# Regrouping the attention cycles of a fused transformer block: five cycles of six or seven exponentials per group in place of six of five or six

## The chip, the cores and the metric

The kernel runs on one core of one Trainium2 chip. The metric is the time of one execution on the device, in microseconds (us). Three runs of the kernel before took 1409.46, 1410.82 and 1412.63 us, so the median is 1410.82 us.

The engines are named as the profile names them: PE is TensorE's matmul, PEld its weight load, ACT is ScalarE, DVE is VectorE, POOL is GpSimd and SP is SyncE, which here only issues DMAs.

## The reference

The reference is one pre-norm transformer block on 2048 rows of width 512: attention with 32 query heads of width 16 that share a single key head and a single value head, then a gated feed-forward part with 1792 hidden columns.

```python
h  = x + A(layernorm(x), wq, wk, wv, wo)
h2 = h + B(layernorm(h), w_gate, w_up, w_down)

def A(x, wq, wk, wv, wo):            # q: 32 heads of 16; one k, one v of width 16
    scores = einsum("bhqd,bkd->bhqk", q, k) * 16 ** -0.5
    p = softmax(scores)
    return merge_heads(einsum("bhqk,bkd->bhqd", p, v)) @ wo

def B(x, w_gate, w_up, w_down):
    return (gelu(x @ w_gate) * (x @ w_up)) @ w_down     # tanh form of gelu
```

## The kernel before, in words

The 2048 query rows are cut into four blocks of 512 (`NB`, `T`), the 32 heads into eight groups of four (`NG`), the 2048 keys into sixteen chunks of 128 (`KC`). For one block, one group and one key chunk, the kernel makes the 128 x 512 scores of four heads, takes their exponential into a tile `p` (128 x 4 x 512), and adds `v` times `p` into an accumulator `acc` that holds the four heads of the group.

PE work of the attention comes in two kinds. A **score** (`scores`, line 431) is a pair of matmuls for two heads: the two run at once on the two halves of PE's rows, and one ACT instruction (line 435) turns the 128 x 1024 result into half of a `p` tile. So a chunk needs two scores and two exponentials, and a group needs 32 of each. A **weighing** (`weigh`, line 439) takes one whole `p` tile and adds it into `acc`: four products on four column strips of PE, 32 columns wide. In PSUM there are two score tiles (tag `s`, two banks each), one bank for `acc`, and three banks for other products. Score number n therefore can't begin until exponential n - 2 has left the score tile that it reuses. There are five `p` tiles (`PB = 5`).

While the scores of block b + 1 are made, the same loop also makes the **dense products** of block b: the output projection, the layer norm's transposes, the gate, up and down products. A generator (`dense`) yields after every dense step, and the loop asks for steps. In the main part of it (`weave`, line 949) a step is again a pair of matmuls, one on each half of PE's rows.

The order on PE, ACT, DVE and SP is the order in which the program is written. It is made by the loop at line 1165, which goes through **cycles**. A cycle emits a few scores, with a written number of dense steps behind each (`shares`), and ends with the weighings of all `p` tiles that are complete (`finish`, line 1021): those whose last exponential isn't the one just issued, and at a group's end all that are left. `SIZES` holds the number of scores of the six cycles of a group, 6, 5, 5, 6, 5 and 5. In the long middle stretch of a block (kind `"woven"`) the shares are these; the last row is that of a group's last cycle:

```python
WOVEN = {6: (0, 6, 3, 3, 2, 0), 5: (0, 6, 3, 2, 0)}
LAST = (0, 6, 4, 2, 0)
```

`(0, 6, 3, 3, 2, 0)` reads: two scores, six dense steps, a score, three steps, a score, three steps, a score, two steps, a score, then the weighings. A block has 36 woven cycles; ahead of them stand four `"long"` ones and a `"gap"`, behind them four `"long"` and two `"short"` ones.

At a cycle's end `open_gates` puts the tanh of a finished gate product (line 826) into ACT's order, and one entry of `outs` (the division of a finished group) goes to `lazy`. `soon` and `lazy` hold DVE instructions; one of them is emitted behind each score (line 1192).

Of the kernel before, what the change touches and what calls it, by code (L numbers as in the profile page):

```python
# [54 lines left out]
RUNS = ((0, 1, 2, 3), (4, 5, 6, 7), (8, 9, 10, 11), (12, 13))  # L55

BOUND_STEPS = ((0, 10), (0, 14))

CUT, EDGE, GAP, HOLD, REST = -1, -2, -3, -4, -5

# [2 lines left out]
def kernel(  # L63
# [21 lines left out]
    NB = S // T  # L85
# [3 lines left out]
    NG = H // 4  # L89
    KC = S // P  # L90
# [69 lines left out]
    def attend(first):  # L160
        with ExitStack() as outer:
            with tc.manual_schedule(
                engines={mybir.EngineType.PE, mybir.EngineType.Pool, mybir.EngineType.Activation}
            ):
                run(outer, first)


    def run(outer, first):
# [268 lines left out]
        def weigh(acc, p, kc):  # L437
            for j in range(4):
                nc.tensor.matmul(  # L439
                    acc[32 * j : 32 * j + 32, :], v_sb[:, kc, :], p[:, j, :],  # L440
                    start=(kc == 0), stop=(kc == KC - 1), skip_group_check=True,
                )
# [3 lines left out]
        def take_out():  # L446
            for step in outs.pop(0):
                step()
# [570 lines left out]
        pend = []  # L1019

        def finish(n):
            for _ in range(min(n, len(pend))):
                pb, pg, pkc, pp, pacc, _ = pend.pop(0)
                weigh(pacc, pp, pkc)
                if pkc == KC - 1:
                    evacuate(pb, pg, pacc)
# [5 lines left out]
        def open_gates():  # L1032
            while gates:
                gates.pop(0)()
# [9 lines left out]
        def score(n, beside=()):  # L1044

            nonlocal acc
            i, u = divmod(n, 2)
            b, r = divmod(i, PER)
            g, kc = divmod(r, KC)
            if u == 0:  # L1050
                if kc == 0:
                    cur["qg"] = qgs.pop((b, g))
                    acc = pss.tile([P, T], F32, tag="acc", bufs=1, name=f"acc_{b}_{g}")
                if kc == 2 and b * NG + g + 1 < NB * NG:
                    key = divmod(b * NG + g + 1, NG)
                    qgs[key] = load_q(*key)
                cur["p"] = sb.tile([P, 4, T], F32, tag="p", bufs=PB, name=f"p_{i}")
            scores(i, cur["p"], cur["qg"], kc, u, beside)
            if u == 1:
                pend.append((b, g, kc, cur["p"], acc, n))  # L1060
# [9 lines left out]
        SIZES = (6, 5, 5, 6, 5, 5)  # L1070

        LEAD = (3, 2, 2)
        n, lead = 0, 2 * PER + sum(SIZES[: LEAD[0]])
        with tc.manual_schedule(engines={mybir.EngineType.SP, mybir.EngineType.DVE}):
# [79 lines left out]

        WOVEN = {6: (0, 6, 3, 3, 2, 0), 5: (0, 6, 3, 2, 0)}
        LAST = (0, 6, 4, 2, 0)
        kinds = (
            ["long"] * 4 + ["gap"] + ["woven"] * 6 * len(SIZES) + ["long"] * 4 + ["short"] * 2
        )
        todo = list(kinds)  # L1160
        fixed = ExitStack()
        fixed.enter_context(
            tc.manual_schedule(engines={mybir.EngineType.SP, mybir.EngineType.DVE})
        )
        for c in range(LEAD[0], (NB - 1) * NG * len(SIZES)):
            b, cb = divmod(c, NG * len(SIZES))
            if first and (b, cb) in BOUND_STEPS:
                bound_flag(BOUND_STEPS.index((b, cb)))
            cg = cb % len(SIZES)
            size, kind = SIZES[cg], None  # L1170
            if b > 0 and cb == LEAD[b]:
                assert work is None
                work, todo = dense(b), list(kinds)
            if work is not None:
                kind = todo.pop(0)
            if kind == "long":
                shares = LONG[size]
            elif kind == "woven":
                shares = LAST if cg == len(SIZES) - 1 else WOVEN[size]
            elif kind == "short":  # L1180
                shares = SHORT[size]
            else:
                shares = PLAIN[size]
            due, said = 0, None
            if kind != "woven":
                while lazy:
                    lazy.pop(0)()
            for j, share in enumerate(shares):
                score(n)
                n += 1  # L1190
                if soon or lazy:
                    (soon or lazy).pop(0)()  # L1192

                if b > 0 and cb == 1 and j == 3 and outs:
                    take_out()

                if kind in (None, "gap") and n % 2 == 0:
                    finish(sum(e[5] < n - 1 for e in pend))
                if kind == "gap" and j == 1:

                    said = next(work)
                due += share
                while due > 0:
                    said = next(work)
                    if said > 0:
                        due -= 1
                    elif said == CUT and kind != "short":
                        break

            ends = kind not in (None, "woven") or kind == "woven" and todo[0] != "woven"  # L1210
            while ends and said not in (CUT, GAP):
                said = next(work)
                assert said < 0, said
            open_gates()
            if work is not None and not todo:
                assert next(work, None) is None
                work = None
            finish(sum(e[5] < n - 1 for e in pend) if cg < len(SIZES) - 1 else len(pend))
            while behind:
                behind.pop(0)()  # L1220
            if outs and kind == "woven":
                lazy.extend(outs.pop(0))
            elif outs:
                take_out()
# [266 lines left out]
    def bound_flag(step):  # L1491
        if step == 0:
            nc.gpsimd.dma_start(b2, b_d)
            return
        nc.vector.tensor_reduce(b1, b2, axis=AX.X, op=ALU.max)

        nc.vector.tensor_scalar(flag, b1, (BOUND_MAX / SCALE) ** 2, None, op0=ALU.is_le)
# [69 lines left out]
```

## Time and profile before

| what | value |
|---|---|
| median of three runs | 1410.82 us (1409.46 to 1412.63) |
| span of the profiled execution, first to last instruction | 1408.1 us |
| PE busy, share of the span | 1391.7 us, 99% |
| ACT busy | 1041.2 us, 74% |
| DVE busy | 552.7 us, 39% |
| score pairs, exponentials | 1024 of each |
| groups 2 to 6 of block 2 (from 700.05 to 901.98 us) | 201.93 us for five groups |

The profile is that of one execution; its own time is known as its span, 1408.1 us, which leaves out what lies ahead of the first instruction and behind the last. The span is 1.4 us under the fastest of the three runs and 2.7 us under their median. PE's matmuls are pipelined and the profile models their ends, so "busy" on PE doesn't mean that PE works at its peak: the starts of successive matmuls say how long a step took. A line such as `s<-qg,kaug` names the tile written and the tiles read; `50*128` behind it are the rows and columns of PE that the matmul holds.

### The profile page before, as it was taken

The page shows a single profiled execution, that of the slowest core. Times are in us where ns is not written, and L with a number is a line of the kernel's source. Part 1 is how long each engine was busy: PE and PEld are TensorE (multiplying, and loading weights), DVE is VectorE, ACT ScalarE, POOL GpSimd, SP SyncE. Part 2 cuts the span into 40 slices and gives each one's busy share as a digit, 9 for nine tenths or more (in the row PEclk, how much of TensorE's full clock was granted, in tenths as well). Part 3 has the DMA queues.
Part 4 walks back from the last instruction along what each step waited for, and adds up shares of the span by engine and source line. Part 5 has one row for each costly group of instructions (what it writes and reads, how often), then busy time and mean ns, then how long its engine had stood idle before and what let it go on. Part 6 is the DMA issues. An engine that isn't in the chain of part 4 may idle for free.

```text
span 1408.1 us, 25648 instructions
## 1 busy us (share of the span) xinstructions
PE 1391.7 (99%) x10646; PEld 782.7 (56%) x10646; DVE 552.7 (39%) x982; ACT 1041.2 (74%) x1149; POOL 189.4 (13%) x288
## 2 busy tenths in 40 slices
PE   8999999999999999999999999999999999999998
PEld 7433333335555555555555655555555555557886
DVE  7322323333342434333252433424352342427665
ACT  7699999996777787777787777777787777772000
POOL 6655565501000000000000000001000000002000
PEclk9999999999999999999999999999999999999999
DMA  4578777842341322233252332223242241335551
GB/s 160 162 238 273 236 243 243 298 134 91 126 150 53 124 106 102 73 112 122 84 169 72 117 118 87 87 100 111 99 151 97 88 147 56 134 124 198 181 199 59
DMA packets 85041, 194.52 MB, mean 138 GB/s; under 512 B 9904, under 2 KB 24240, under 8 KB 84884
## 3 DMA queue, kind: packets, MB, share of 16 engines
q1 hardware_dynamic: 77484, 167.39, 35.3%
q0 software_dynamic: 7264, 25.30, 5.0%
q8 instruction: 86, 1.41, 0.4%
q14 instruction: 39, 0.32, 0.1%
q10 hardware_dynamic: 168, 0.10, 0.0%
HBM read 142.93 MB, written 49.55 MB: 137 GB/s over the span
## 4 chain that ended last, share of the span: by engine, by line
PE 93%; ACT 3%; DMA 1%; issue 1%; DVE 1%; POOL 0%; SPq 0%; ACTq 0%; DVEq 0%; POOLq 0%
PE acc L439 33%; PE s L431 19%; PE pu L949 9%; PE pg L949 8%; PE pd L949 4%; PE pq L429 4%; PE pd L626 3%; ACT p L435 3%; PE pd L648 3%; PE pg L648 3%; PE pu L648 3%; PE pp L626 2%; PE pp L757 1%; DMA x<-in_A_x_dram 1%; PE pxt L693 1%
## 5 line engine op out<-in xcount | busy, mean ns | idle before, releaser
L435 ACT ACTIVATE p<-s 128x1024 f32<-128x1024 f32 x1024 | 969.7, 1030 | 224.6 <-PE s L431 220.1
L439 PE MATMUL acc<-p,v_sb 128*32 128x512 f32 x4096 | 496.4, 600 | 0.0
L431 PE MATMUL s<-qg,kaug 50*128 50x512 f32 x1984 | 416.3, 423 | 3.7 <-ACT p L435 3.6
L431 PEld LDWEIGHTS s<-qg,kaug 50*128 50x128 f32 x1984 | 194.6, 184 | 217.8 <-ACT p L435 120.6
L439 PEld LDWEIGHTS acc<-p,v_sb 128*32 128x32 f32 x4096 | 109.8, 109 | 229.2 <-issue 226.0
L949 PE MATMUL pu<-x2h,w 64*128 64x512 f32 x672 | 211.8, 391 | 0.0
L949 PE MATMUL pg<-x2h,w 64*128 64x512 f32 x672 | 211.5, 391 | 0.1
L949 PEld LDWEIGHTS pu<-x2h,w 64*128 64x128 f32 x672 | 115.8, 185 | 15.1
L949 PEld LDWEIGHTS pg<-x2h,w 64*128 64x128 f32 x672 | 116.2, 185 | 12.6 <-DVE g L823 0.5
L949 PE MATMUL pg<-x2l,w 64*128 64x512 f32 x336 | 122.2, 391 | 0.0
L949 PE MATMUL pu<-x2l,w 64*128 64x512 f32 x336 | 121.8, 390 | 0.0
L826 ACT ACTIVATE ga<-ga 128x512 f32<-128x512 f32 x56 | 35.3, 634 | 89.2 <-DVE ga L821 89.2
L139 POOL TENSOR_SCALAR rstd<-mv 128x1 f32<-128x1 f32 x16 | 3.5, 221 | 666.4 <-DVE mv L137 666.4
L949 PE MATMUL pd<-w,gh 64*128 64x512 f32 x384 | 81.3, 392 | 0.0
L891 DVE TENSOR_TENSOR h<-h,pd 128x512 f32<-128x512 f32 x48 | 31.9, 685 | 115.4 <-PE pd L949 66.4
L1192 DVE SCALAR_TENSOR_TENSOR ga<-ga,g 128x512 f32<-128x512 f32 x70 | 48.3, 691 | 52.3 <-ACT ga L826 51.2
L452 DVE COPY oT<-acc 128x512 f32<-128x512 f32 x32 | 22.1, 692 | 112.1 <-PE acc L439 111.9
L479 DVE RECIPROCAL oc<-oc 128x128 f32<-128x128 f32 x64 | 56.3, 921 | 24.3 <-DMA oc<-acc_d 19.5
L810 DVE COPY g<-pg 128x512 f32<-128x512 f32 x56 | 38.8, 692 | 62.8 <-PE pg L949 57.0
L949 PEld LDWEIGHTS pu<-x2l,w 64*128 64x128 f32 x336 | 57.9, 185 | 7.6
L949 PEld LDWEIGHTS pg<-x2l,w 64*128 64x128 f32 x336 | 58.1, 185 | 6.1
L823 DVE SCALAR_TENSOR_TENSOR g<-g,pu 128x512 f32<-128x512 f32 x56 | 38.2, 683 | 40.4 <-PE pu L949 30.4
(248 smaller groups left out, 1462.4 us busy)
## 6 DMA issues: line engine op xcount, KB each, us to landing
w<-w_d SPq DMA_DIRECT2D x112, 512.0 KB
w<-w_d SPq DMA_DIRECT2D x28, 1024.0 KB
qg<-q_d SPq DMA_DIRECT2D x46, 200.0 KB
q_d<-qh SPq DMA_DIRECT2D x32, 256.0 KB
wo<-wo_d SPq DMA_DIRECT2D x8, 1024.0 KB
acc_d<-oT SPq DMA_DIRECT2D x31, 256.0 KB
oc<-acc_d SPq DMA_DIRECT2D x124, 64.0 KB
w_d<-w_0b POOLq DMA_DIRECT2D x14, 512.0 KB, 7.6
```

Of the source, the lines that this page charges most:

```text
L429: step()
L431: nc.tensor.matmul(s[:, a, :], kaug[rows, kc * P : (kc + 1) * P], qg[rows, 2 * u + a, :], start=True, stop=True,)
L435: nc.scalar.activation(p[:, 2 * u : 2 * u + 2, :], s, AF.Exp, scale=SCALE)
L439: nc.tensor.matmul(acc[32 * j : 32 * j + 32, :], v_sb[:, kc, :], p[:, j, :], start=(kc == 0), stop=(kc == KC - 1), skip_group_check=True,)
L479: nc.vector.reciprocal(oc[:, 1, sl], oc[:, 1, sl])
L626: nc.tensor.matmul(banks[k], lhsT[rows], rhs[rows], start=(turn == 0 and i == 0), stop=(turn == 1 and i == n - 1), skip_group_check=True,)
L648: nc.tensor.matmul(bank, lhsT, rhs, start=(i == 0), stop=(i == len(ts) - 1))
L810: nc.vector.tensor_copy(g, pg)
L823: nc.vector.scalar_tensor_tensor(g, g, 0.5, pu, op0=ALU.mult, op1=ALU.mult)
L826: nc.scalar.activation(a, a, AF.Tanh, scale=GELU_A * GELU_C)
L949: nc.tensor.matmul(e["bank"], lhsT[rows], rhs[rows], start=i == 0 and not e["both"], stop=last and e["both"], skip_group_check=True,)
L1192: (soon or lazy).pop(0)()
```

## The change

The change touches five of the eight groups in each of blocks 1 to 3, numbered from 0: groups 2 to 6 (`FULL`). For those, a group is cut into five cycles of 7, 6, 7, 6 and 6 scores, with the dense steps given by the new table `WIDE`. Their number per group stays: 73 before (14 + 11 + 11 + 14 + 11 + 12) and 73 now (16 + 13 + 16 + 14 + 14). Groups 0, 1 and 7 keep their six cycles. The number of woven cycles of a block falls from 36 to 31, and a cycle's place in its group comes from a list (`rows`) in place of a division.

```diff
+FULL = range(2, 7)
...
         WOVEN = {6: (0, 6, 3, 3, 2, 0), 5: (0, 6, 3, 2, 0)}
         LAST = (0, 6, 4, 2, 0)
+        WIDE = (
+            (0, 4, 3, 3, 3, 3, 0), (0, 4, 3, 3, 3, 0), (0, 4, 3, 3, 3, 3, 0),
+            (0, 5, 3, 3, 3, 0), (0, 5, 3, 3, 3, 0),
+        )
+        assert sum(map(len, WIDE)) == 2 * KC
+        rows = []
+        for g in range(NG):
+            sizes = [len(w) for w in WIDE] if g in FULL else SIZES
+            rows.extend(
+                (g, cg, size, cg == len(sizes) - 1) for cg, size in enumerate(sizes)
+            )
+        spare = len(SIZES) - len(WIDE)
         kinds = (
-            ["long"] * 4 + ["gap"] + ["woven"] * 6 * len(SIZES) + ["long"] * 4 + ["short"] * 2
+            ["long"] * 4 + ["gap"] + ["woven"] * (6 * len(SIZES) - spare * len(FULL))
+            + ["long"] * 4 + ["short"] * 2
         )
...
-        for c in range(LEAD[0], (NB - 1) * NG * len(SIZES)):
-            b, cb = divmod(c, NG * len(SIZES))
+        for c in range(LEAD[0], (NB - 1) * len(rows)):
+            b, cb = divmod(c, len(rows))
...
-            cg = cb % len(SIZES)
-            size, kind = SIZES[cg], None
+            g, cg, size, final = rows[cb]
+            kind = None
...
-                shares = LAST if cg == len(SIZES) - 1 else WOVEN[size]
+                shares = WIDE[cg] if g in FULL else LAST if final else WOVEN[size]
...
-            finish(sum(e[5] < n - 1 for e in pend) if cg < len(SIZES) - 1 else len(pend))
+            finish(len(pend) if final else sum(e[5] < n - 1 for e in pend))
```

Two places show what this does to PE's order, both in the first cycle of group 2 of block 2 (the one that begins at 700.05 us in the profile before). `s_` are score matmuls (x2 is one score), `pg_` and `pu_` are gate and up products (two rows are one dense step), `acc_` are weighings (x4 is one `p` tile).

The first place is the stretch between the second and the third score of the cycle. Before, its last five dense steps and the third score:

```order
L949 MATMUL pg_2_7461<-x2h_6866,w_1_4_7377 128x512
L949 MATMUL pu_1_7435<-x2h_6866,w_1_3_6874 128x512
L949 MATMUL pg_2_7461<-x2l_6867,w_1_4_7377 128x512
L949 MATMUL pu_1_7435<-x2l_6867,w_1_3_6874 128x512
L949 MATMUL pg_2_7461<-x2h_6866,w_1_4_7377 128x512
L949 MATMUL pu_1_7435<-x2h_6866,w_1_3_6874 128x512
L949 MATMUL pg_2_7461<-x2h_6866,w_1_4_7377 128x512
L949 MATMUL pu_1_7435<-x2h_6866,w_1_3_6874 128x512
L949 MATMUL pg_2_7461<-x2l_6867,w_1_4_7377 128x512
L949 MATMUL pu_1_7435<-x2l_6867,w_1_3_6874 128x512
L431 MATMUL s_0_7590<-qg_2_7216,kaug 128x512 x2
```

And now, the second score, four steps and the third score:

```order
L433 MATMUL s_1_7571<-qg_2_7216,kaug 128x512 x2
L951 MATMUL pu_2_7508<-x2h_6866,w_1_5_7403 128x512
L951 MATMUL pu_1_7435<-x2h_6866,w_1_3_6874 128x512
L951 MATMUL pg_2_7461<-x2h_6866,w_1_4_7377 128x512
L951 MATMUL pu_1_7435<-x2h_6866,w_1_3_6874 128x512
L951 MATMUL pg_2_7461<-x2l_6867,w_1_4_7377 128x512
L951 MATMUL pu_1_7435<-x2l_6867,w_1_3_6874 128x512
L951 MATMUL pg_2_7461<-x2h_6866,w_1_4_7377 128x512
L951 MATMUL pu_1_7435<-x2h_6866,w_1_3_6874 128x512
L433 MATMUL s_0_7586<-qg_2_7216,kaug 128x512 x2
```

The third score, which waits for the cycle's first exponential, stands two dense steps earlier.

The second place is the end of that cycle. Before, it ends with its sixth score, behind two dense steps, and weighs two tiles:

```order
L949 MATMUL pg_2_7461<-x2h_6866,w_1_4_7377 128x512
L949 MATMUL pu_2_7508<-x2h_6866,w_1_5_7403 128x512
L949 MATMUL pg_3_7628<-x2h_6866,w_1_6_7451 128x512
L949 MATMUL pu_2_7508<-x2h_6866,w_1_5_7403 128x512
L431 MATMUL s_1_7631<-qg_2_7216,kaug 128x512 x2
L439 MATMUL acc_2_7565<-p_7566,v_sb 32x512 x4
L439 MATMUL acc_2_7565<-p_7589,v_sb 32x512 x4
L431 MATMUL s_0_7646<-qg_2_7216,kaug 128x512 x2
```

Now:

```order
L951 MATMUL pg_3_7633<-x2h_6866,w_1_6_7451 128x512
L951 MATMUL pu_2_7508<-x2h_6866,w_1_5_7403 128x512
L433 MATMUL s_0_7641<-qg_2_7216,kaug 128x512 x2
L441 MATMUL acc_2_7565<-p_7566,v_sb 32x512 x4
L441 MATMUL acc_2_7565<-p_7585,v_sb 32x512 x4
L441 MATMUL acc_2_7565<-p_7612,v_sb 32x512 x4
L433 MATMUL s_1_7659<-qg_2_7216,kaug 128x512 x2
```

The cycle ends with a seventh score, the first half of a fourth `p` tile, behind three dense steps, and weighs three tiles. Over the group the tiles weighed at the ends of the cycles were 2, 3, 2, 3, 3, 3 and are now 3, 3, 3, 3, 4. Line numbers behind the new constants are higher by two.

## Prediction

> **What bounds the kernel now.** I read the profile's page first, then the chain of waits, then the timeline of single cycles. The page says which engine is full.
>
> ```profile
> span 1408.1 us, 25648 instructions
> PE 1391.7 (99%) x10646; PEld 782.7 (56%) x10646; DVE 552.7 (39%) x982; ACT 1041.2 (74%) x1149; POOL 189.4 (13%) x288
> PEclk9999999999999999999999999999999999999999
> PE 93%; ACT 3%; DMA 1%; issue 1%; DVE 1%; POOL 0%; SPq 0%; ACTq 0%; DVEq 0%; POOLq 0%
> L435 ACT ACTIVATE p<-s 128x1024 f32<-128x1024 f32 x1024 | 969.7, 1030 | 224.6 <-PE s L431 220.1
> L431 PEld LDWEIGHTS s<-qg,kaug 50*128 50x128 f32 x1984 | 194.6, 184 | 217.8 <-ACT p L435 120.6
> ```
>
> PE is full, its clock isn't throttled, and the chain that ends last is 93% PE. ACT works 74% of the time, so over the whole span it could follow PE easily. But the last row shows that weight loads of scores waited 120.6 us in total for exponentials. That is no loss yet, since a load may wait while PE streams earlier matmuls, but it says that the two engines run close to each other somewhere. The place is inside a cycle, which the timeline shows. First PE, in the first cycle of a group:
>
> ```profile
> 700.05 0.73 PE L431 MATMUL s<-qg,kaug 50*128 50x512 f32 x4
> 700.62 0.40 PE L949 MATMUL pu<-x2h,w 64*128 64x512 f32 x2
> ...
> 702.01 0.39 PE L431 MATMUL s<-qg,kaug 50*128 50x512 f32 x2
> ...
> 702.93 0.40 PE L431 MATMUL s<-qg,kaug 50*128 50x512 f32 x2
> ...
> 703.86 0.39 PE L431 MATMUL s<-qg,kaug 50*128 50x512 f32 x2
> ...
> 704.55 0.46 PE L431 MATMUL s<-qg,kaug 50*128 50x512 f32 x2
> 704.94 1.92 PE L439 MATMUL acc<-p,v_sb 128*32 128x512 f32 x16
> 706.79 0.73 PE L431 MATMUL s<-qg,kaug 50*128 50x512 f32 x4
> ```
>
> From the starts: six dense steps take 702.01 - 700.62 = 1.39 us, 0.232 each; a score with three steps behind it takes 0.925 (702.01 to 703.86 is two of them); the two scores at the head take 0.57, which is 0.11 over two times 0.23; weighing two tiles takes 1.85. Now ACT over this cycle and the next two, which begin on PE at 706.79 and 713.47:
>
> ```profile
> 700.68 5.62 ACT L435 ACTIVATE p<-s 128x1024 f32<-128x1024 f32 x6 [1.94 <-PE s L431]
> 706.18 0.63 ACT L826 ACTIVATE ga<-ga 128x512 f32<-128x512 f32 x1
> 707.39 4.71 ACT L435 ACTIVATE p<-s 128x1024 f32<-128x1024 f32 x5 [0.58 <-PE s L431]
> 714.01 2.88 ACT L435 ACTIVATE p<-s 128x1024 f32<-128x1024 f32 x3 [1.39 <-PE s L431]
> ```
>
> The first exponential starts 0.63, 0.60 and 0.54 us after the cycle's first score (0.54 where the cycle begins with the second half of a `p` tile). The six then run back to back: (5.62 - 1.03) / 5 = 0.918 from one start to the next. So within a cycle ACT has no slack at all: a score with three steps takes PE 0.925 and an exponential takes ACT 0.918. ACT idles only while PE weighs (1.94, 0.58 and 1.39 us). What keeps PE ahead is the head of the cycle: ACT starts 0.6 late, and six dense steps give it time for that.
>
> **What a cycle costs beside its content.** The saving can be read from another cycle's end and the chain's own pieces.
>
> ```profile
> 717.04 0.40 PE L431 MATMUL s<-qg,kaug 50*128 50x512 f32 x2
> 717.38 0.64 PE L439 MATMUL acc<-p,v_sb 128*32 128x512 f32 x4
> 724.18 2.71 PE acc L439 x24
> ```
>
> A last score is followed by the weighing after 0.34 instead of 0.23 (704.55 above took 0.39; its own wait comes below). Three tiles take 2.71 and two 1.85, so a tile takes 0.86 and a batch has 1.85 - 2 x 0.86 = 0.13 of its own. With the 0.11 at the head, a cycle costs 0.11 + 0.10 + 0.13 = 0.34 beyond its scores, steps and tiles. The change removes one cycle from each of 15 groups: **-0.34 per group, -5.1 us**. Scores, exponentials, dense steps and weighings keep their numbers.
>
> **What a score that waits costs.** In the rows above no score waited long enough to delay PE much, so I need one that did.
>
> ```profile
> 1005.68 2.85 ACT L435 ACTIVATE p<-s 128x1024 f32<-128x1024 f32 x3 [0.20 <-ACT p L435]
> 1006.76 0.19 PEld L431 LDWEIGHTS s<-qg,kaug 50*128 50x128 f32 x2 [0.28 <-ACT p L435]
> 1006.76 0.50 PE L431 MATMUL s<-qg,kaug 50*128 50x512 f32 x2
> 1007.10 0.39 PE L949 MATMUL pu<-x2l,w 64*128 64x512 f32 x1
> ...
> 1007.68 0.50 PE L431 MATMUL s<-qg,kaug 50*128 50x512 f32 x2
> 1008.11 0.64 PE L439 MATMUL acc<-p,v_sb 128*32 128x512 f32 x4
> ```
>
> The first of the three exponentials ends at 1005.68 + 1.03 = 1006.71. The score that needs its tile starts 0.05 later, and the dense step behind it 0.34 after that instead of 0.23, since the weights could only be loaded then. So what follows a waiting score starts no earlier than 0.39 after the end of the exponential. The second one (1007.68 to 1008.11, 0.43 where 0.34 is free) says the same. At 717.04 the score is 0.15 behind the end of its exponential (714.01 + 2.88 = 716.89) and pays nothing; at 704.55 it is 0.09 behind (700.68 + 3 x 0.918 + 1.03 = 704.46) and pays 0.05. Of the six old cycles four begin with a whole `p` tile and have two steps ahead of their last score, like the latter.
>
> **The new cycles, step by step** (times from the cycle's first score).
>
> With four steps, the third score would come at 0.57 + 4 x 0.232 = 1.50. The first exponential ends at 0.63 + 1.03 = 1.66 in the group's first cycle, at 1.57 in the second and third, which begin with half a tile. PE waits: the step behind the third score starts at 1.66 + 0.39 = 2.05 (1.96) instead of 1.73, **a loss of 0.32 (0.23)**. With five steps, in the last two cycles, the score comes at 1.73, 0.10 behind the end at 0.60 + 1.03 = 1.63; the step behind it starts at 2.02 instead of 1.96, a loss of 0.06. The old six steps put the score at 1.96, free of this. After that the fourth score comes 0.34 + 3 x 0.232 = 1.03 after the third, 0.16 behind the end of its exponential (1.08 less 0.92), like the score at 717.04, and each later one gains 0.925 - 0.918: no further loss.
>
> - 7 scores, first cycle: third score 1.71, fourth 2.74, seventh 2.74 + 3 x 0.925 = 5.515, weighing + 0.33, three tiles + 2.71: 8.555.
> - 6 scores, four steps: 1.62, 2.65, sixth 4.50; 7.54.
> - 7 scores, third cycle: 1.62, 2.65, seventh 5.425; 8.465.
> - 6 scores, five steps: the fourth score at 2.02 + 0.695 = 2.715, the sixth 4.565; 7.605.
> - the last: the same, with four tiles (2.71 + 0.86): 8.465.
>
> Together **40.63 us per group**. Before, five groups took the time between these starts:
>
> ```profile
> 700.05 0.73 PE L431 MATMUL s<-qg,kaug 50*128 50x512 f32 x4
> 901.98 0.50 PE L431 MATMUL s<-qg,kaug 50*128 50x512 f32 x2
> ```
>
> That is 201.93 / 5 = 40.39 per group. So **+0.24 per group and 15 x 0.24 = +3.6 us**: 0.34 saved, some 0.2 saved at the old cycle ends, and 0.90 lost at five third scores (0.32 + 2 x 0.23 + 2 x 0.06). The five losses are the uncertain term. Below: if a waiting score delayed PE only to its start (0.05 after the exponential) and the late load cost nothing, the losses are 0.21, 0.12, 0.12, 0 and 0, 0.45 together, and a group takes 40.18, -3.1 us over all. Above: if each of the 17 later scores of a group also paid the 0.05 of the row at 704.55, +0.85 per group, +16 us. I take the first reading, since the rows at 1006.76 and 1007.68 are the very case, and 717.04 speaks against the upper end.
>
> A rule of the Trainium skill, from its page ScalarE: Activation LUTs (What ACT_TABLE_LOAD costs), would make the pace worse: an ACTIVATE with immediate operands takes 186 ns plus 0.833 ns per element, less 93 ns of overlap back to back, 0.946 us for 1024 elements. By it an exponential is slower than a score with three steps, each of 17 later scores would wait about 0.02, and the sum would be near +9 us; the 0.918 of this trace decides against it.
>
> **What costs nothing.** DMAs: the load of the next group's `qg` and the weight loads hang on the fifth score and on dense steps, which keep their numbers per group. `p` tiles: at most four are in use in a cycle, and each one that is reused was weighed at the end of an earlier cycle, so the five suffice. Weighing: the youngest tile of a batch starts 2 x 0.86 after the first, when its exponential has long ended (in the first cycle at about 0.63 + 5 x 0.918 + 1.03 = 6.25, against 5.845 + 1.72 = 7.57). The tanh at a cycle's end takes 0.63; the first wide cycle leaves ACT 8.555 + 0.60 - 7.17 = 1.99 us for it. If one falls between two exponentials of a wide cycle, up to 0.63 would be PE's; by the order of ACT's instructions five do (three before), each behind the fourth exponential of six or the fifth of seven, and no score left in that cycle waits for an exponential that comes after it. DVE, 39% busy, gets one deferred instruction per score as before.
>
> **Rivals.**
>
> *The switches win.* A program with 15 cycles less saves 0.34 x 15 = 5.1 us, and 0.2 x 15 = 3 more if the late loads at the old ends vanish with nothing in their place: 1405.7 to 1402.7. For it speaks that the saving is certain, against it that four steps (1.50) are less than 1.57 to 1.66. It decides if the first exponential ends before about 1.35, which needs ACT to start 0.32 after the first score; three cycles show 0.54 to 0.63. This is also what a rule of the Trainium skill by itself gives: TensorEngine Tiling (Array Packing), Key Properties, says that changing the tiling mode drains TensorE. The rows agree that the change between score and weighing costs time, 0.34 a cycle.
>
> *It cancels.* If the late load costs about half of what the row shows, or the old ends lose more than I count, a group comes out between 40.2 and 40.57 and the run within 2.8 us of before: about 1411.
>
> *ACT becomes the bound.* The wide cycles run 0.007 per score from ACT's pace. If an exponential is late within a cycle (before the one at 1005.68 ACT idled 0.20 with its score ready; a tanh waits for DVE), all later scores inherit it, where before the sequence ended sooner. 0.2 more per group gives +6.6 us, 1417.4; it decides if the fourth to seventh scores of the wide cycles also wait.
>
> That the change doesn't do what it says is excluded by the order: the groups have five batches of weighings.
>
> **How the numbers follow.** The span of 1408.1 becomes 1411.7. The span is 2.7 us under the median of the runs, so I add the difference to the median: 1410.82 + 3.6 = **1414.4**. Chances: the forecast 0.53, by itself 1412.4 to 1416.4; it cancels 0.20; ACT the bound 0.15; the switches win 0.12. The range leaves out most of the last and the far end of the third: 1408.5 to 1418.5. About 0.2%, 2.8 us, is what a measurement here tells from no change. Slower by more: most of the forecast (0.43) and the third, 0.58; within: the rest of the forecast and the second, 0.30; faster 0.12.
>
> **What would show it.** In the timeline, the third score of a cycle of group 2 starts 1.62 to 1.71 after the first (1.96 before), and the step behind it 0.34 later; with the five steps at 1.73. A group lasts 40.5 to 40.7. The weight loads of scores wait more than 120.6 us for exponentials. Groups 0, 1 and 7 keep their times. I am wrong if the third scores start at 1.50 (the switches win), or if later scores of a cycle are more than 0.95 apart (ACT the bound).

## The result and the profile after

The changed kernel takes 1420.25 us (median of five runs, 1418.48 to 1423.23) against 1410.82 us (1409.46 to 1412.63) before: **9.4 us slower, a ratio of 1.0068 with a 95% interval of 1.0058 to 1.0079**. The direction was forecast; the size was 2.6 times the forecast's 3.6 us, and the time lies above its range of 1408.5 to 1418.5.

These are rows of the page after, in the order of the ones shown of before.

```profile
span 1421.5 us, 25635 instructions
PE 1401.7 (99%) x10646; PEld 767.1 (54%) x10646; DVE 549.7 (39%) x982; ACT 1034.2 (73%) x1149; POOL 191.3 (13%) x288
L437 ACT ACTIVATE p<-s 128x1024 f32<-128x1024 f32 x1024 | 962.7, 1038 | 242.6 <-PE s L433 238.2
L433 PEld LDWEIGHTS s<-qg,kaug 50*128 50x128 f32 x1984 | 194.1, 184 | 239.1 <-ACT p L437 111.5
L951 PE MATMUL pg<-x2h,w 64*128 64x512 f32 x672 | 212.5, 392 | 2.9 <-DMA w<-w_d 2.9
```

The last row's counterpart on the page before:

```profile
L949 PE MATMUL pg<-x2h,w 64*128 64x512 f32 x672 | 211.5, 391 | 0.1
```

The number of instructions on PE and ACT is the same and PE is as full as ever; it just takes longer. Gate products now waited 2.9 us for the DMA of their weights, where the row before shows no such wait. The wait of the scores' weight loads for exponentials fell from 120.6 to 111.5 us, where the prediction had it rise: this sum over the whole span mixes loads that wait under running matmuls with loads that hold PE up, and doesn't show the loss. The profiled execution is the slowest of the five (1423.23); of the 13.4 us by which its span is longer, 1.7 lie in the first group of block 0, which the change doesn't touch.

The first wide cycle of group 4 of block 2, in PE's timeline:

```profile
786.67 0.74 PE L433 MATMUL s<-qg,kaug 50*128 50x512 f32 x4
...
788.38 0.50 PE L433 MATMUL s<-qg,kaug 50*128 50x512 f32 x2
788.72 0.40 PE L951 MATMUL pg<-x2h,w 64*128 64x512 f32 x1
...
789.43 0.40 PE L433 MATMUL s<-qg,kaug 50*128 50x512 f32 x2
...
790.37 0.40 PE L433 MATMUL s<-qg,kaug 50*128 50x512 f32 x2
...
791.31 0.40 PE L433 MATMUL s<-qg,kaug 50*128 50x512 f32 x2
...
792.24 0.40 PE L433 MATMUL s<-qg,kaug 50*128 50x512 f32 x2
792.56 2.78 PE L441 MATMUL acc<-p,v_sb 128*32 128x512 f32 x24
795.28 0.74 PE L433 MATMUL s<-qg,kaug 50*128 50x512 f32 x4
```

The third score starts 1.71 us after the first and the step behind it at 2.05, as predicted to the hundredth. The later scores stand 0.94, 0.94 and 0.93 apart instead of 0.925, and the cycle takes 8.61 against the 8.555 of the sum.

Four groups without any other disturbance, 3 to 6 of block 2, begin and end at these scores; the pair of rows is after. The single row is the beginning before, whose end, at 901.98, was shown in the prediction.

```profile
745.86 0.73 PE L433 MATMUL s<-qg,kaug 50*128 50x512 f32 x4
...
909.12 0.73 PE L433 MATMUL s<-qg,kaug 50*128 50x512 f32 x4
```

```profile
740.35 0.73 PE L431 MATMUL s<-qg,kaug 50*128 50x512 f32 x4
```

163.26 / 4 = 40.81 against 161.63 / 4 = 40.41: **+0.41 per group**, where the sum said +0.24. Over 15 groups that is 6.1 us. The other groups of these blocks, 0, 1 and 7, keep their times within 0.06 us.

The rest is in group 2, the first wide group of a block. It takes 41.10, 41.64 and 45.02 us in blocks 1, 2 and 3 (40.27, 40.30 and 40.30 before). In block 3 its second cycle runs into a weight load. First SP's queue and the product concerned, after:

```profile
1037.47 4.44 SPq L588 DMA_DIRECT2D w<-w_d  x2
...
1045.98 0.46 PE L951 MATMUL pg<-x2h,w 64*128 64x512 f32 x1 [2.33 <-DMA w<-w_d]
```

And the same load and the same product (the first step of the gate product `pg_4`) in block 2 before:

```profile
706.01 3.05 SPq L586 DMA_DIRECT2D w<-w_d  x2
...
714.04 0.39 PE L949 MATMUL pg<-x2h,w 64*128 64x512 f32 x1
```

Both loads are issued 5.96 us after their group's first score. Before, the product came 8.03 us after the issue, since the old second cycle ended and weighed three tiles just ahead of it. Now it stands in the middle of the second cycle, behind nine steps, and PE reached it near 1043.5, 6.0 us after the issue; it started at 1045.98, 8.5 after. In block 2 after, the same product waited 0.59 and started 6.74 us after the issue:

```profile
710.18 4.44 SPq L588 DMA_DIRECT2D w<-w_d  x2
...
716.92 0.47 PE L951 MATMUL pg<-x2h,w 64*128 64x512 f32 x1 [0.59 <-DMA w<-w_d]
```

So at the 6.74 us of block 2 the old order's 8.03 would have been enough and the new order's 6.0 isn't. In block 3 the load also took longer, and with 8.5 us it would have been late by about 0.5 in the old order too; why it took longer there isn't known. What followed the wait shows in the windows around it (busy time of each engine, then the granted clock, the DMA share and the rate):

```profile
1043.48:1046.00 2.52, 0.19 (x4) 0.06 (x2) 1.22 (x3) 0.95 (x2) 0.00 (x0) 1.00 1.02 398
1046.00:1050.00 4.00, 4.00 (x24) 1.89 (x28) 0.29 (x1) 2.57 (x3) 0.00 (x0) 0.63 0.28 114
```

PE did almost nothing for 2.5 us while the DMA engines were full (398 GB/s), and in the 4 us behind that its granted clock was 0.63.

### The profile page after: what moved, and what is told of

Same layout as the page of the kernel before. It is cut to its first block, busy times and chain, and to the rows that moved or that the text cites. A ratio compares the mean times of both kernels' runs of the same rounds, so it can differ in the third digit from the quotient of the medians.

```text
span 1421.5 us, 25635 instructions
## 1 busy us (share of the span) xinstructions
PE 1401.7 (99%) x10646; PEld 767.1 (54%) x10646; DVE 549.7 (39%) x982; ACT 1034.2 (73%) x1149; POOL 191.3 (13%) x288
## 4 chain that ended last, share of the span: by engine, by line
PE 92%; ACT 4%; DMA 2%; issue 1%; POOL 0%; DVE 0%; SPq 0%; ACTq 0%; DVEq 0%; POOLq 0%
PE acc L441 33%; PE s L433 19%; PE pu L951 8%; PE pg L951 8%; PE pd L951 5%; PE pq L431 4%; ACT p L437 4%; PE pd L628 3%; PE pd L650 3%; PE pg L650 3%; PE pu L650 3%; PE pp L628 2%; DMA w<-w_d 1%; DMA x<-in_A_x_dram 1%; PE pp L759 1%; PE pxt L695 1%
## 5 line engine op out<-in xcount | busy, mean ns | idle before, releaser
L433 PEld LDWEIGHTS s<-qg,kaug 50*128 50x128 f32 x1984 | 194.1, 184 | 239.1 <-ACT p L437 111.5
L1207 DVE SCALAR_TENSOR_TENSOR ga<-ga,g 128x512 f32<-128x512 f32 x74 | 51.2, 692 | 47.0 <-ACT ga L828 45.4
L481 DVE RECIPROCAL oc<-oc 128x128 f32<-128x128 f32 x64 | 56.5, 923 | 18.1 <-DMA oc<-acc_d 13.4
```

The lines of the kernel that those rows point to most:

```text
L433: nc.tensor.matmul(s[:, a, :], kaug[rows, kc * P : (kc + 1) * P], qg[rows, 2 * u + a, :], start=True, stop=True,)
L481: nc.vector.reciprocal(oc[:, 1, sl], oc[:, 1, sl])
```

## The experiments

Each kernel was timed against the kernel before on its chip: 1410.26 us for the first four, 1410.55 for the next three, 1410.09 for the last two. Group times are from the first score of group 3 to that of group 7 in block 2, divided by four: 40.41 before and 40.81 in the change.

**Six steps at every head, still five cycles.** Is it the early third score alone, or the whole wide cycle?

```diff
-            (0, 4, 3, 3, 3, 3, 0), (0, 4, 3, 3, 3, 0), (0, 4, 3, 3, 3, 3, 0),
-            (0, 5, 3, 3, 3, 0), (0, 5, 3, 3, 3, 0),
+            (0, 6, 3, 3, 2, 2, 0), (0, 6, 3, 2, 2, 0), (0, 6, 3, 3, 2, 2, 0),
+            (0, 6, 3, 3, 2, 0), (0, 6, 3, 3, 2, 0),
```

> Five cycles of 7, 6, 7, 6, 6 scores as in the change, but each with six dense steps at its head and the steps taken from its end: (0,6,3,3,2,2,0), (0,6,3,2,2,0), (0,6,3,3,2,2,0), (0,6,3,3,2,0) twice. Theory 'ACT bounds the whole cycle': a cycle's last score can't start before the end of the exponential two ahead of it, 0.60 + (k - 3) x 0.918 + 1.03 after the cycle's first score for k exponentials, wherever the steps stand. The third scores wait for nothing, the last ones wait instead (about 0.13 in the cycles of seven and the second one), and a group still takes 40.7 to 40.8 us against 40.8 in the change and 40.4 before; the run lies at 1416 to 1420. Theory 'only the four-step head': the 0.8 us of third-score waits per group vanish with nothing in their place, a group takes 40.0 to 40.1, the run about 1406.

Measured: 1422.54 us, ratio 1.0090 (1.0071 to 1.0109), group time 40.89: the run is 2.5 us above its range, and the mean holds one group of 41.27, whose excess isn't placed, beside three of 40.74 to 40.81. Products waited 3.5 us for weights in this run's trace too, in two waits. The wait for exponentials has moved to the cycle's end, as these rows of a first wide cycle show (its first score, its exponentials, its end):

```profile
785.25 0.74 PE L433 MATMUL s<-qg,kaug 50*128 50x512 f32 x4
785.87 6.56 ACT L437 ACTIVATE p<-s 128x1024 f32<-128x1024 f32 x7 [2.81 <-PE s L433]
...
790.29 0.40 PE L951 MATMUL pu<-x2l,w 64*128 64x512 f32 x1
790.66 0.49 PE L433 MATMUL s<-qg,kaug 50*128 50x512 f32 x2
791.09 2.78 PE L441 MATMUL acc<-p,v_sb 128*32 128x512 f32 x24
```

The last score starts 0.37 behind the step ahead of it instead of 0.23, and the weighing follows after 0.43 instead of 0.33. So the loss isn't a flaw of four-step heads alone. The last of seven scores needs the tile of the fifth exponential, which by the prediction's rows ends no sooner than 0.63 + 4 x 0.918 + 1.03 = 5.33 us after the first score, wherever the sixteen steps stand; PE alone would be there at 0.57 + 20 x 0.232 = 5.21, and here it got there at 5.41. Heads of five steps in the cycles of seven weren't run.

**A repeated score in the change.** If PE stands still at the third score, more work there is free.

```diff
+            for a in range(2) if twice else ():      # the second score of a four-step cycle, again
+                rows = slice(64 * a, 64 * a + KR)
+                nc.tensor.matmul(s[:, a, :], kaug[rows, ...], qg[rows, 2 * u + a, :], start=True, stop=True)
```

> The change, with the second score of each four-step cycle (the first three cycles of the 15 wide groups) issued twice, into the same score tile with the same values: 45 pairs of matmuls more, 45 x 0.232 = 10.4 us of PE work. If PE stands still there because it waits for the first exponential (0.31 and twice 0.23 lost per group), the extra pair is done in that time: 0 to +1 us against the change, group time unchanged at 40.8. If PE were the bound there and the time is lost elsewhere: +10.4 us, 0.7 per wide group.

Measured: 1419.09 us, ratio 1.0072 (1.0047 to 1.0097), against the change's 1.0068. The two medians alone don't settle it, since no product waits for weights in this run's trace (two wait for DVE instead, 1.8 us together). The group time does: from these first scores of groups 3 and 7 it is 163.31 / 4 = 40.83, against 40.81 in the change and 41.5 if each pair had cost its 0.232.

```profile
744.61 0.73 PE L433 MATMUL s<-qg,kaug 50*128 50x512 f32 x4
...
907.92 0.73 PE L433 MATMUL s<-qg,kaug 50*128 50x512 f32 x4
```

The extra pairs cost nothing that can be measured. The first wide cycle of a group, with the repeated score at 785.99:

```profile
785.42 0.73 PE L433 MATMUL s<-qg,kaug 50*128 50x512 f32 x4
785.99 0.39 PE L439 MATMUL s<-qg,kaug 50*128 50x512 f32 x2
...
787.15 0.48 PE L433 MATMUL s<-qg,kaug 50*128 50x512 f32 x2
787.47 0.40 PE L957 MATMUL pg<-x2h,w 64*128 64x512 f32 x1
```

The third score now starts 1.73 us after the first, and the step behind it at 2.05, exactly where it stands in the change (788.72 less 786.67).

**The same repeated scores in the kernel before**, as a control.

> Control for the run before it: the same 45 repeated scores in the first three cycles of groups 2 to 6 of the kernel before, which have six steps at their head. There PE doesn't wait at the third score, so the pairs cost their 0.232 each, less the 0.05 that two of the three cycles now lose at their last score: 0.6 per group, +8.5 to +10.4 us, 1419.5 to 1421. If repeated scores are free anywhere, 0.

Measured: 1421.43 us, ratio 1.0079 (1.0063 to 1.0096): +11.2 us, a little over the range. Its trace has 1.1 us of waits of dense products for weights and DVE beside the pairs. The group time is 41.25; three of the four groups, which none of these waits touches, take 40.97 to 41.10, 0.65 more than before, or 0.22 per pair. Where nothing waits the pairs cost their time.

**The change in groups 3 to 6 alone.**

```diff
-FULL = range(2, 7)
+FULL = range(3, 7)
```

> The change in groups 3 to 6 alone; group 2 keeps its six cycles. Theory 'weights late in group 2': in the change's profile group 2 of blocks 2 and 3 lost 0.8 and 4.7 us in its second cycle, where a gate product waited for its weights, because the packed steps of the first wide cycle call for them sooner than their load lands. With group 2 as before there is no such wait, and the rest costs 12 x 0.42 = 5.1 us: 1415.5 to 1416.5. Rival, the first wide group pays wherever it is: group 3 now shows the wait, 1418 or more.

Measured: 1416.00 us, ratio 1.0039 (1.0025 to 1.0054), +5.7. Group 2 is back at 40.27 to 40.31 and groups 3 to 6 take 40.8, except 41.12 in group 4 of block 2 and 42.03 in group 4 of block 3, where the list of waits has the only one left for weights:

```profile
PE pg L951 <- DMA w<-w_d: 1.0, 1, 1.0
```

The time fits, but the theory's "no such wait" doesn't: a smaller wait has come up in another group. So it isn't tied to the first wide group. That it comes wherever a product falls too soon behind its load, and so depends on how the steps are dealt out, is the likely reading; this run doesn't show it by itself.

**Five weight buffers in the change**, so that each load is asked for one product earlier.

```diff
-W1 = 4
+W1 = 5
```

> The change with five buffers for the gate and up weights instead of four, so that each weight load is asked for one product earlier. Theory 'weights late in group 2': no matmul of group 2 waits for a weight load, its clock isn't cut behind that wait, and groups 2 to 6 all take 40.8: 15 x 0.42 = 6.3 us over before, 1417 (the change 1420.3). Rival, the loads are late because the DMA engines are full then, whenever they are asked for: 1420.

Measured: 1416.51 us, ratio 1.0039 (1.0024 to 1.0054), +6.0 us. No matmul waits for a weight load, all 15 wide groups take 40.78 to 40.90, and group 2 of block 3 takes 1073.34 - 1032.44 = 40.90:

```profile
1032.44 0.74 PE L433 MATMUL s<-qg,kaug 50*128 50x512 f32 x4
...
1073.34 0.73 PE L433 MATMUL s<-qg,kaug 50*128 50x512 f32 x4
```

So of the 9.4 us some 3.5 belong to late weights and what follows them, and 6.0 to the cycles themselves, 0.40 per group. The 3.5 is a difference of two medians, each known to 1.5 to 2 us; the 6.0 is borne out by the groups, 15 x 0.41 = 6.1. (The profiled execution, 1420.10, is the slowest of this run's four: it loses 3.7 us ahead of block 1, where two scores waited 2.1 us for the DMA of `qg`.)

**Seven cycles**, the other direction.

```diff
+            (0, 5, 3, 3, 0), (0, 6, 4, 0), (0, 5, 3, 3, 0), (0, 6, 4, 0),
+            (0, 5, 3, 2, 0), (0, 6, 4, 0), (0, 5, 3, 3, 0),
```

> The other direction: seven cycles of 5, 4, 5, 4, 5, 4, 5 scores in groups 2 to 6, with (0,5,3,3,0), (0,6,4,0), (0,5,3,3,0), (0,6,4,0), (0,5,3,2,0), (0,6,4,0), (0,5,3,3,0), 73 steps as ever. Theory 'six cycles balance PE and ACT': now PE is the bound in every cycle, waits for exponentials fall, and one more cycle costs its 0.34 per group less the 0.2 of late loads at the old ends: +0.14 to +0.2 per group, +2 to +3 us, 1412.5 to 1413.5. If a cycle's own 0.34 were not real: the 0.2 saved alone, 1407.5. If fewer cycles are worse because more cycles are better: below 1406.

Measured: 1420.59 us, ratio 1.0073 (1.0053 to 1.0092), +10.0, group time 40.87. All three expectations missed. I had written five-step heads without working their cost out. The fifth cycle of a group shows two places:

```profile
811.38 0.73 PE L433 MATMUL s<-qg,kaug 50*128 50x512 f32 x4
...
813.10 0.46 PE L433 MATMUL s<-qg,kaug 50*128 50x512 f32 x2
...
814.10 0.39 PE L433 MATMUL s<-qg,kaug 50*128 50x512 f32 x2
...
814.88 0.49 PE L433 MATMUL s<-qg,kaug 50*128 50x512 f32 x2
815.31 2.78 PE L441 MATMUL acc<-p,v_sb 128*32 128x512 f32 x24
```

The fourth score comes 1.00 behind the third instead of 0.925, and the last one 0.78 behind the fourth instead of 0.695, with its weighing 0.43 later. These are the waits of the prediction again. 15 x 0.46 is 6.9 us. In the profiled execution (1421.94) the 15 groups lose 8.2 us in all, and 3.6 us are lost ahead of block 1, in a part that the edit doesn't touch: two scores wait there for the DMA of `qg` (1.12 us at 234.32 and 1.29 us at 237.01), and over the 4 us from 237 us on the granted clock was 0.57.

**Other cycle lengths, six per group.** The old cycles lose 0.05 at four ends; can it be had?

```diff
+            (0, 6, 4, 2, 0), (0, 6, 3, 3, 2, 0), (0, 6, 3, 3, 2, 0),
+            (0, 6, 2, 0), (0, 6, 3, 3, 2, 0), (0, 6, 3, 2, 0),
```

> Six cycles again in groups 2 to 6, but of 5, 6, 6, 4, 6, 5 scores: all cycles but the first begin with the second half of a tile, whose exponential starts 0.54 instead of 0.60 after the cycle's first score, and the shares (0,6,4,2,0), (0,6,3,3,2,0) twice, (0,6,2,0), (0,6,3,3,2,0), (0,6,3,2,0) keep each score 0.15 or more behind the exponential it needs. Theory 'a late weight load costs 0.05 at four cycle ends of the old group': up to 0.2 less per group, -2 to -3 us, 1407.5 to 1409, group time 40.2. If these late loads cost nothing: 1410.3, no change.

Measured: 1417.69 us, ratio 1.0054 (1.0038 to 1.0070), above both expectations. Groups 3 to 6 take 40.37, no gain worth the name. The second cycle begins on PE at 791.43 with the second half of a tile:

```profile
791.97 5.69 ACT L437 ACTIVATE p<-s 128x1024 f32<-128x1024 f32 x6 [1.05 <-PE s L433]
```

```profile
795.24 0.39 PE L433 MATMUL s<-qg,kaug 50*128 50x512 f32 x2
...
795.93 0.46 PE L433 MATMUL s<-qg,kaug 50*128 50x512 f32 x2
796.31 2.78 PE L441 MATMUL acc<-p,v_sb 128*32 128x512 f32 x24
```

ACT does start at 0.54, but then an exponential takes (5.69 - 1.03) / 5 = 0.93 from start to start, not 0.918: behind six-step heads the scores come 0.93 apart, and ACT, once it has caught up with them, can't go faster. So its early start is lost by the fourth exponential, and the last score still pays 0.05 (0.38 to the weighing). The 7.1 us come from group 2 (42.23, 42.46 and 44.34 against 40.30), where products waited 1.9 us for weights and 3.7 us for DVE.

**One batch more in the kernel before**: the price of changing between scores and weighing, alone.

```diff
                 score(n)
                 ...
+                if 2 <= cb // 6 < 7 and cg == 3 and j == 2:
+                    finish(1)
```

> The kernel before, with one weighing batch more in groups 2 to 6: in the fourth cycle of a group the oldest complete tile is weighed alone behind the third score, and the cycle's end weighs two tiles instead of three. Scores, steps and tiles keep their numbers and nothing waits for an exponential there, so this is the price of a change between scores and weighing and back by itself. By the rows of the prediction 0.34 per batch, less up to 0.05 of a late load at that cycle's end: 0.29 to 0.34 per group, 15 x = +4.4 to +5.1 us, 1415 to 1415.6. If the price is only what a batch has of its own (0.13): +2 us, 1412.5.

Measured: 1415.15 us, ratio 1.0040 (1.0024 to 1.0056): +5.1 us for 15 batches, 0.34 each by the medians; the group time, 40.70, says 0.29. These are the two ends of the expected range. The price can be read around the lone tile:

```profile
804.46 0.40 PE L431 MATMUL s<-qg,kaug 50*128 50x512 f32 x2
804.79 1.07 PE L439 MATMUL acc<-p,v_sb 128*32 128x512 f32 x8
805.78 0.50 PE L949 MATMUL pu<-x2l,w 64*128 64x512 f32 x1
806.12 0.39 PE L949 MATMUL pu<-x2h,w 64*128 64x512 f32 x1
```

0.33 to the tile (0.23 between steps), 0.99 for the tile (0.86 within a batch), 0.34 from the first step behind it to the second: 0.10 + 0.13 + 0.11.

**Seven cycles with six steps at each head**, and five weight buffers.

```diff
+            (0, 6, 3, 2, 0), (0, 6, 4, 0), (0, 6, 3, 2, 0), (0, 6, 3, 0),
+            (0, 6, 3, 2, 0), (0, 6, 4, 0), (0, 6, 3, 2, 0),
```

> Seven cycles of 5, 4, 5, 4, 5, 4, 5 scores in groups 2 to 6 again, now with six steps at every head, (0,6,3,2,0), (0,6,4,0), (0,6,3,2,0), (0,6,3,0), (0,6,3,2,0), (0,6,4,0), (0,6,3,2,0), and five weight buffers. The seven cycles of the run before lost 0.1 at third scores behind five steps and 0.2 at an end behind two short stretches; with these gone only the price of one more cycle stays: +0.3 per group against before, 40.7, +4.5 us, 1415. If seven cycles were slower for another reason, the groups stay at 40.9 and the run at 1417.5 or more.

Measured: 1414.80 us, ratio 1.0036 (1.0023 to 1.0049), +4.7; group time 40.61. With the waits gone, a seventh cycle costs 0.20 per group, less than the 0.34 of one change; what gives the rest back wasn't followed up. No kernel tried beats the one before.

## Why the prediction was wrong, and where it was right

- **What a cycle costs** (0.34 by the rows): right. The extra batch measured it by itself, 0.29 to 0.34 each.
- **What a score that waits costs**: right. In group 3 of block 2 the steps behind the five third scores start at 2.05, 1.96, 1.97, 2.02 and 2.02 us, within 0.01 of the sum. The repeated score shows that PE stands still there: three pairs per group are free in the change and cost 0.65 us in the kernel before.
- **The new cycles, step by step**: the mechanism held, a term was mis-sized. The five cycles of that group take 8.59, 7.58, 8.50, 7.64 and 8.51 us, 0.18 more together than the sum's 40.63. "Each later one gains 0.925 - 0.918: no further loss" should have read 0.94 apart (0.936 is the mean in groups 3 to 6 of block 2). 17 later scores at 0.01 each make the 0.17 between +0.24 and +0.41, and 2.5 us over 15 groups. One cycle had given me the 0.925. It isn't a price of waiting alone, since old cycles have 0.93 too (the scores at 762.50 and 763.43 us, for one). Why the steps of the new cycles run 1% slower isn't settled; ACT's pace, 0.915 in these cycles, isn't the limit. The sum was also loose in two ways: it set a summed new group against a measured old one, for which the same rows give 40.35 and not 40.39, and the terms that it lists, -0.34, -0.2 and +0.90, come to +0.36 and not to +0.24.
- **What costs nothing, DMAs**: this step failed. I argued that weight loads hang on dense steps "which keep their numbers per group". The number per group doesn't matter; what matters is the time between a load's issue and the step that reads it. The wide cycles put nine steps of the second cycle ahead of a weighing that had given the load 8.0 us, and left it 6.0, where it needed 6.7 in block 2 and 8.5 in block 3. That cost about 3.5 us at the median, by the run with five buffers, and is what took the time out of the range: 3.6 + 2.5 + 3.5 is 9.6, and 9.4 was measured. Two lists stood in what I had: the rows of SP's queue, and PE's order with the names of the weight tiles.
- **The rivals.** "The switches win": the price of changing between scores and weighing is real here (0.34 a cycle) and was saved; the waits cost more. The Trainium skill's page TensorEngine Tiling (Array Packing), Key Properties, has the rule that a change of tiling mode drains TensorE. The run with one batch more agrees that the change costs time; that a drain is the cause isn't shown by any run. "ACT becomes the bound" did not happen by its own sign: the later scores stand 0.936 us apart on average, where the sign asked for more than 0.95. That its price, 1417.4, is near the 1416.5 without late weights is chance. But it asked the right question: a cycle of seven has a floor set by ACT, as the run with six-step heads shows.
- **The 0.946 us per exponential.** The estimate worked out from the Trainium skill's page ScalarE: Activation LUTs (What ACT_TABLE_LOAD costs) isn't what these traces show: seven exponentials take 6.52 us in the change, (6.52 - 1.03) / 6 = 0.915 from start to start. That its +9 us is near the result is chance: the run with five weight buffers has these same cycles and no late weights, and stands at +6.0.

```profile
787.30 6.52 ACT L437 ACTIVATE p<-s 128x1024 f32<-128x1024 f32 x7 [2.93 <-PE s L433]
```

## What to carry to other kernels

When two engines feed each other through two buffers and a third kind of work interrupts them in batches, each cycle has two floors, one per engine. Fewer and longer cycles save the price of the interruption but raise the other engine's floor, and with 73 steps per group six cycles is the best of the orders tried here (five cost 0.40 us per group more, seven 0.20 more). Before calling a prefetch free because its count is unchanged, write down, for each load that is reused soon, the time from issue to first use in the old order and in the new.

## What was not expected of the hardware

A short stop of PE can cost more than its own length. In the change the wait of 2.33 us for weights was followed by 4 us at a granted clock of 0.63. In that stretch a batch of weighing that otherwise takes 2.78 us took 3.99:

```profile
1047.97 3.99 PE L441 MATMUL acc<-p,v_sb 128*32 128x512 f32 x24
```

In the run with six-step heads a wait of 2.40 us for weights was followed by 4 us at 0.70. But the run with other cycle lengths has three stops of nearly one length, and the 4 us behind them were at 1.00, 1.00 and 0.61:

```profile
386.83 0.50 PE L951 MATMUL pg<-x2h,w 64*128 64x512 f32 x1 [1.68 <-DVE g L825]
...
714.87 0.47 PE L951 MATMUL pg<-x2h,w 64*128 64x512 f32 x1 [1.87 <-DMA w<-w_d]
...
1041.33 0.47 PE L951 MATMUL pg<-x2h,w 64*128 64x512 f32 x1 [1.99 <-DVE oc L481]
```

So the cut doesn't follow every such stop, and what decides isn't shown here.
